# The seams into two Strassen stages of a mixer kernel: one batch kept by a copy, fewer sums, low parts on another engine

## The chip, the core and the metric

The program runs on one core of one Trainium2 chip. The metric is the time of one execution in device microseconds (us). Of the kernel before there are three timed runs and one profiled execution. In the text PE is TensorE, DVE is VectorE, ACT is ScalarE, POOL is GpSimd and SP is SyncE, whose queue issues nearly all DMAs here.

## What is computed

Attention over 4 batches of 448 tokens (12 heads of 64), then two mixers on the result, in 32-bit floats:

```python
attn = softmax(rmsnorm(q) @ rmsnorm(k).T / 8) @ v
x = attn, heads side by side                 # 4 batches of 448 x 768
u = x + (U V) mixing of the tokens           # first mixer, rank 32
x = u + relu(u @ w_ch1) @ w_ch2              # 768 -> 3072 -> 768
u = x + relu(x^T @ w_tok1) @ w_tok2          # second mixer, over tokens
out = u + relu(u @ w_ch1) @ w_ch2            # 768 -> 1536 -> 768
```

## The kernel before, in words

To keep 32-bit accuracy on the fast matmul path every operand is held as two tiles, a high part (its rounded copy) and a low part (what the rounding left). A product takes three matmuls: high by high, low by high, high by low. `split` makes the two parts: ACT copies the value to the high part, then POOL subtracts (lines 143 to 145).

The work is done in two halves: batches 0 and 1 first, then 2 and 3. This case concerns the second half, where `pair_ffn` runs the channel part of a mixer for two batches together, once for the first mixer (its name is `"a"`, 24 chunks of hidden width) and once for the second (`"b"`, 12 chunks). "Batch 0" of the change means the first of the two, `xs[0]`; `xs[1]` is the other. Both hold u transposed, 128 partitions by 6 chunks of 448 tokens. `us[0]` and `us[1]` are the split copies of the same u, named `uh, ul` and `vh, vl` inside the function. The result of each group of hidden chunks is added to `xs` in place (`second`, line 645 before), so `xs` no longer holds u once the first group is through.

Hidden chunks go two at a time (G = 2). The first group and the last are computed plainly: `plain` makes the hidden activations (tile `ps_g`, then the relu into `gs`), `second` multiplies them with the second weights (tile `ps_x`) and adds to `xs`. The groups between use Strassen's scheme over a 2 by 2 block matrix, the two batches being one dimension: `seven` makes seven products (tile `ps_p`) in place of eight. For that it needs

- four combinations of the two u, T1 to T4, once per stage (`sums`, tiles `t1` to `t4`, each with a high and a low part): T1 = u1a - u0a, T2 = u1b - T1, T3 = u1b - u1a, T4 = u0b - T2, where 0 and 1 are the batches and a and b the halves of the channels;
- four combinations of the two weight chunks, once per group (`w1_blocks`, from line 212): DVE makes the sums (lines 223 to 226, tile `w_t`), `split` makes the parts (tiles `w_a` and `w_s`).

In `sums` before, u of `xs[1]` is taken from `xs[1]` itself, while u of `xs[0]` is put together from `uh` and `ul`, since `xs[0]` has been changed by then. That costs a second operation in T1 and in T4:

```python
nc.vector.tensor_sub(t1, x[:, c], f(uh[:, c]))
nc.vector.tensor_sub(t1, t1, f(ul[:, c]))
```

The scheduler of the framework reorders what the code says: it places each engine's instructions by its own estimate of when they could run, so the order on each engine is a result, and it differs from the order of the lines. Each engine then works strictly through its list. Two places are called seams below: **seam A**, where the last batch's rank mix ends and stage "a" begins (about 1010 to 1072 us of the span), and **seam B**, where the token mix ends and stage "b" begins (about 1400 to 1458 us).

PSUM is shared out by pools: `m` has 3 buffers, `s` 2, `t` 1 and `p` 2. `ps_g` takes from `m`, and `ps_x` in `pair_ffn` in turn from `m` and `p`. A buffer of `ps_x` is freed by the DVE addition to `xs`.

Of the kernel before, what the change touches and what calls it, by code (L numbers as in the profile page):

```python
# [10 lines left out]
F32R = mybir.dt.float32r  # L11
U32 = mybir.dt.uint32
I64 = mybir.dt.int64
AF = mybir.ActivationFunctionType
# [10 lines left out]
def attention_then_two_mixers(  # L25
# [30 lines left out]
    nc = tc.nc  # L56
    P = 128
    B, H, S, D = q.shape
# [8 lines left out]
    G = 2  # L67
# [4 lines left out]
    act = ctx.enter_context(tc.tile_pool(name="act", bufs=2))  # L72
    dram = ctx.enter_context(tc.tile_pool(name="dram", bufs=1, space=DRAM))

    def f(x):
        return x.bitcast(F32)

    def mm(o, l, r, start, stop):
        nc.tensor.matmul(o, lhsT=l, rhs=r, start=start, stop=stop)  # L79
# [20 lines left out]
    pools = {"late": False}  # L100
# [7 lines left out]
    def psum(kind, shape, name):  # L108
        pool = pools[kind]
        return pool.tile(shape, F32, tag=pool.name, name=name)  # L110
# [32 lines left out]
    def split(w, hi, lo):  # L143
        nc.scalar.activation(hi, w, AF.Copy)  # L144
        nc.gpsimd.tensor_sub(lo, w, f(hi))  # L145
# [63 lines left out]
    def tmp():  # L209
        return pools["pu"].tile([P, S], F32, tag="pu", name="pu")  # L210
# [346 lines left out]
    def pair_ffn(nm, w1, w2, xs, us, after, half=None):  # L557

        n = w1.shape[1] // P
        HC = CC // 2  # L560
        (uh, ul), (vh, vl) = us

        def sums():


            ts = [act.tile([P, 2, HC, S], F32R, tag="xT", name="t1")]
            ts += [pools["tb"].tile([P, 2, HC, S], F32R, tag=f"t{i}", name=f"t{i}")
                   for i in (2, 3, 4)]
            x = xs[1]
            for c in range(HC):  # L570
                t1, t2, t3, t4 = [tmp() for _ in range(4)]
                nc.vector.tensor_sub(t1, x[:, c], f(uh[:, c]))
                nc.vector.tensor_sub(t1, t1, f(ul[:, c]))
                nc.vector.tensor_sub(t2, x[:, HC + c], t1)
                nc.gpsimd.tensor_sub(t3, x[:, HC + c], x[:, c])
                nc.vector.tensor_sub(t4, f(uh[:, HC + c]), t2)
                nc.vector.tensor_add(t4, t4, f(ul[:, HC + c]))
                for t, v_ in zip(ts, (t1, t2, t3, t4)):
                    split(v_, t[:, 0, c], t[:, 1, c])
            return {f"t{i + 1}": (t[:, 0], t[:, 1]) for i, t in enumerate(ts)}  # L580

        def plain(u, ws):
            pg = psum("m", [P, S], "ps_g")
            wh, wl = ws
            for cc in range(CC):
                fs = slice(cc * P, (cc + 1) * P)
                mm(pg, wh[:, fs], u[0][:, cc], cc == 0, False)
                mm(pg, wl[:, fs], u[0][:, cc], False, False)
                mm(pg, wh[:, fs], u[1][:, cc], False, cc == CC - 1)
            return relu(pg)  # L590

        def relu(ps):
            s = pools["g"].tile([P, 2, S], F32R, tag="g", name="gs")
            gh, gl = s[:, 0], s[:, 1]
            nc.scalar.activation(gh, ps, AF.Relu)  # L595
            nc.vector.scalar_tensor_tensor(
                gl, ps, 0.0, f(gh), op0=ALU.max, op1=ALU.subtract
            )
            return gh, gl
# [37 lines left out]
        def second(xT, gs, ws, done=None):  # L637
            for dc in range(CC):
                px = psum("mp"[dc % 2], [P, S], "ps_x")
                ds = slice(dc * P, (dc + 1) * P)  # L640
                for i, ((gh, gl), (wh, wl)) in enumerate(zip(gs, ws)):
                    mm(px, wh[:, ds], gh, i == 0, False)
                    mm(px, wl[:, ds], gh, False, False)
                    mm(px, wh[:, ds], gl, False, i == len(gs) - 1)
                nc.vector.tensor_add(xT[:, dc], px, xT[:, dc])  # L645
                if done and dc % 3 == 2:
                    done(dc // 3)
                yield
# [5 lines left out]
        def chunks(j0):  # L654
            return ([w1_chunk(nm, w1, j0 + i) for i in range(G)],
                    [w2_chunk(nm, w2, j0 + i) for i in range(G)])

        def drain(it):
            for _ in it:
                pass  # L660

        w1s, w2s = chunks(0)
        drain(second(xs[0], [plain(us[0], ws) for ws in w1s], w2s))
        b = sums()
        b.update(b11=(uh[:, :HC], ul[:, :HC]), b21=(uh[:, HC:], ul[:, HC:]),
                 b22=(vh[:, HC:], vl[:, HC:]))
        rest_ = second(xs[1], [plain(us[1], ws) for ws in w1s], w2s)
        for j0 in range(G, n - G, G):
            a = w1_blocks(nm, j0)
            gs = [[None] * 2 for _ in xs]  # L670
            for _ in seven(a, b, gs):
                next(rest_, None)
                next(rest_, None)
            drain(rest_)
            rest_ = seconds(gs, [w2_chunk(nm, w2, j0 + i) for i in range(G)])
        w1s, w2s = chunks(n - G)
# [39 lines left out]
    xs = [new_x() for _ in range(2)]  # L716
    us = [None] * 2
# [4 lines left out]
    wt, kept = [], []  # L722
    with ExitStack() as stack:
# [6 lines left out]
        def new_xo():  # L730
# [4 lines left out]
             for b, xT in zip((b0, b1), xs) for hp in range(NP)]  # L735
            + [(b, hp, (), new_xo,
                lambda dst, b=b, hp=hp: nc.sync.dma_start(xd[b][hp], dst))
# [10 lines left out]
        w1s = [w1_chunk("a", wa1, j) for j in range(G)]  # L748
# [80 lines left out]
```

## Time and profile before

| what | value |
| --- | --- |
| timed runs | 1589.35, 1595.9, 1597.39 us; median 1595.9 |
| profiled execution, its own time | 1591.42 us |
| its span, first to last instruction | 1589.4 us |
| busy: PE, DVE, ACT, POOL | 93%, 72%, 46%, 51% of the span |
| mean granted TensorE clock | 0.981 of full |

A share is busy time over the whole span. PE is busy nearly throughout, but the page's 40 slices show two dips of PE in the second half, in the slices around 1020 us and 1420 us, where POOL is at its fullest. The granted clock is 1.0 (the 2.4 GHz level) or 0.5 (the 1.2 GHz level) at any moment. A mean below 1 says for how much of a stretch the lower level was granted.

### The profile page before, as it was taken

What the parts mean: (1) busy time and instruction counts of PE and PEld (TensorE: products, weight loads), DVE (VectorE), ACT (ScalarE), POOL (GpSimd) and SP (SyncE); (2) the same over time, 40 slices, a digit from 0 to 9 for tenths busy, and PEclk for the clock granted to TensorE, in tenths of its full rate; (3) what the DMA queues carried; (4) which work ended last, traced back from release to release, by engine and by line L of the source; (5) the groups of instructions that cost most, each with busy time, mean ns of one, the idle gap of its engine ahead of it and who ended that gap; (6) DMA issues with size and microseconds to landing.
All of it is one profiled execution on the core that took longest, in us unless ns stands there. A gap on an engine that the chain in (4) does not pass through costs nothing.

```text
span 1589.4 us, 21794 instructions
## 1 busy us (share of the span) xinstructions
PE 1482.6 (93%) x7522; PEld 1283.8 (81%) x7522; DVE 1137.4 (72%) x1949; ACT 730.1 (46%) x1461; POOL 806.4 (51%) x659
## 2 busy tenths in 40 slices
PE   5999987999999999998999999689999999979998
PEld 3556566788779898897888998579999999978997
DVE  6899878998788888667857654755766664475653
ACT  5788755666556665434534334322322321332311
POOL 4567657767556564444745443662343522375320
PEclk9999989999999999999999999889999999999999
DMA  5666553556554453542415423111212111001202
GB/s 150 152 159 163 144 173 112 178 149 204 178 170 148 137 158 108 204 144 86 171 63 199 157 100 118 46 40 50 70 50 69 47 54 52 29 21 50 70 20 90
DMA packets 103373, 178.21 MB, mean 112 GB/s; under 512 B 10400, under 2 KB 79488, under 8 KB 103264
## 3 DMA queue, kind: packets, MB, share of 16 engines
q1 hardware_dynamic: 102944, 176.82, 36.0%
q8 instruction: 60, 0.98, 0.3%
q14 instruction: 49, 0.40, 0.1%
q10 hardware_dynamic: 320, 0.00, 0.0%
HBM read 107.19 MB, written 36.57 MB: 90 GB/s over the span
## 4 chain that ended last, share of the span: by engine, by line
PE 58%; DVE 15%; POOL 5%; issue 4%; DMA 3%; ACT 2%; SPq 0%; DVEq 0%; POOLq 0%; ACTq 0%
PE ps_x L79 26%; PE ps_g L79 14%; PE ps_p L79 11%; POOL w_bits L134 2%; DVE w_bits L131 2%; DVE xT L528 2%; DVE w_bits L126 2%; PE ps_u L79 2%; PE ps_t L79 2%; PE sc L79 1%; PE pv L79 1%; DVE nm L330 1%; DVE w_bits L127 1%; DVE pl L370 1%; PE pt L358 1%
## 5 line engine op out<-in xcount | busy, mean ns | idle before, releaser
L79 PE MATMUL ps_x<-gs,w 128*128 128x448 f32 x2592 | 579.8, 371 | 27.4 <-ACT gs L595 11.2
L79 PEld LDWEIGHTS ps_x<-gs,w 128*128 128x128 f32 x2592 | 484.2, 190 | 76.9 <-DVE xT L528 14.0
L79 PE MATMUL ps_g<-u,w 128*128 128x448 f32 x1584 | 347.3, 371 | 6.6 <-POOL u L438 4.3
L79 PEld LDWEIGHTS ps_g<-u,w 128*128 128x128 f32 x1584 | 295.6, 189 | 34.6 <-POOL u L438 6.3
L134 POOL TENSOR_TENSOR w_bits<-w_bits,w_round 128x768 uint32<-128x768 uint32 (+3 forms) x80 | 143.7, 1797 | 114.8 <-issue 36.3
L145 POOL TENSOR_TENSOR w<-w_bits,w 128x768 fp32r<-128x768 f32 (+3 forms) x82 | 147.7, 1809 | 87.1 <-ACT w L144 82.0
L339 POOL TENSOR_SCALAR p<-p,sm 112x448 f32<-112x448 f32 x192 | 132.0, 701 | 99.5 <-DVE sm L336 37.7
L645 DVE TENSOR_TENSOR xT<-ps_x,xT 128x448 f32<-128x448 f32 x216 | 128.5, 618 | 72.7 <-PE ps_x L79 71.2
L528 DVE TENSOR_TENSOR xT<-ps_x,xT 128x448 f32<-128x448 f32 x216 | 132.2, 617 | 40.3 <-PE ps_x L79 38.4
L145 POOL TENSOR_TENSOR w<-w 128x768 fp32r<-128x768 f32 x44 | 83.5, 1908 | 133.3 <-ACT w L144 109.2
L332 ACT ACTIVATE p<-sc,nm 112x448 f32<-112x448 f32 x192 | 121.6, 637 | 54.3 <-DVE nm L330 48.4
L145 POOL TENSOR_TENSOR w_a<-w_a 128x384 fp32r<-128x384 f32 (+1 forms) x28 | 42.9, 1531 | 167.9 <-DVE w_t L223 124.3
L616 DVE TENSOR_TENSOR pu<-ps_p,pu 128x448 f32<-128x448 f32 x98 | 58.9, 620 | 89.0 <-PE ps_p L79 84.0
L330 DVE TENSOR_REDUCE nm<-sc 112x1 f32<-112x448 f32 x192 | 116.2, 613 | 8.5 <-PE sc L79 7.6
L358 PEld LDWEIGHTS pt<-ident,p 112*112 112x112 f32 x768 | 86.4, 133 | 39.7 <-issue 19.4
L366 ACT ACTIVATE ph<-pt 112x448 fp32r<-112x448 f32 (+1 forms) x192 | 101.6, 546 | 27.1 <-PE pt L358 26.0
L358 PE MATMUL pt<-ident,p 112*112 112x112 f32 x768 | 111.2, 262 | 2.6 <-POOL p L339 1.5
L126 DVE TENSOR_SCALAR w_bits<-w_bits 128x768 f32<-128x768 f32 (+3 forms) x80 | 71.0, 888 | 47.4 <-ACT w_bits L125 47.4
L130 ACT ACTIVATE w_round<-w_raw 128x768 uint32<-128x768 uint32 (+3 forms) x80 | 69.8, 872 | 72.2 <-POOL w_bits L134 67.1
L438 POOL TENSOR_TENSOR u<-xT,u 128x448 fp32r<-128x448 f32 x48 | 61.4, 1289 | 68.7 <-ACT u L437 68.3
L370 DVE TENSOR_TENSOR pl<-pt,ph 112x448 fp32r<-112x448 f32 x144 | 87.4, 613 | 10.0 <-ACT ph L366 9.3
L125 ACT ACTIVATE w_bits<-w_raw 128x768 f32<-128x768 f32 (+3 forms) x80 | 70.0, 875 | 49.9 <-POOL w L145 35.5
(107 smaller groups left out, 2433.1 us busy)
## 6 DMA issues: line engine op xcount, KB each, us to landing
w_raw<-in_moe_w_ch_dram SPq DMA_DIRECT2D x72, 768.0 KB, 4.5
c_a<-w_bits SPq DMA_DIRECT2D x48, 384.0 KB, 3.4
ks<-hi SPq DMA_DIRECT2D x96, 112.0 KB, 2.3
kt<-lo SPq DMA_DIRECT2D x96, 112.0 KB, 2.3
w<-c_a SPq DMA_DIRECT2D x28, 384.0 KB, 3.7
c_b<-w_bits SPq DMA_DIRECT2D x24, 384.0 KB, 3.1
w_a<-c_a SPq DMA_DIRECT2D x20, 384.0 KB, 2.9
w<-c_b SPq DMA_DIRECT2D x16, 384.0 KB, 3.3
```

What stands on the lines that cost most here:

```text
L79: nc.tensor.matmul(o, lhsT=l, rhs=r, start=start, stop=stop)
L126: nc.vector.tensor_scalar_max(f(w), f(w), TINY)
L134: nc.gpsimd.tensor_tensor(w, w, r, op=ALU.add)
L145: nc.gpsimd.tensor_sub(lo, w, f(hi))
L330: nc.vector.tensor_reduce(nm, sc, axis=AX.X, op=ALU.max, negate=True)
L332: nc.scalar.activation(p, sc, AF.Exp, bias=nm, accum_out=sm[:, c % 2:c % 2 + 1])
L339: nc.gpsimd.tensor_scalar(x, x, sm[:, i:i + 1], 1.0, op0=ALU.mult, op1=ALU.mult)
L358: nc.tensor.transpose(pt[:, c * CP:(c + 1) * CP], pr[c][:, kc * CP:(kc + 1) * CP], ident[:CP, :CP],)
L366: nc.scalar.activation(ph, pt, AF.Copy)
L370: nc.vector.tensor_sub(pl, pt, f(ph))
L528: nc.vector.tensor_add(xT[:, dc], px, xT[:, dc])
L645: nc.vector.tensor_add(xT[:, dc], px, xT[:, dc])
```

## The change

Four things, all in `pair_ffn`:

- A new `keep_first` runs ahead of everything else in the stage: two DMAs on SP's queue copy `xs[0]`, as long as it is still u, into the low-part halves of the tiles of T3 and T4 (128 by 1344 floats of 4 bytes each, 672 KB a copy). The low parts proper are written over them later.
- `sums` takes u of batch 0 from that copy. Per channel chunk it has four operations where it had six, so 12 for 18 per stage; T3, which POOL made, is now made by DVE.
- The low parts of T1 to T4 are subtracted by DVE (`part`), no longer by POOL (`split`): 12 operations per stage.
- The first group's `w1_blocks` is called ahead of the plain group, and the plain hidden activations of batch 1 (`g1`) ahead of `sums`.

```diff
+        def keep_first():
+            ts = [pools["tb"].tile([P, 2, HC, S], F32R, tag=f"t{i}", name=f"t{i}") for i in (3, 4)]
+            for h, t in enumerate(ts):
+                nc.sync.dma_start(f(t[:, 1]), xs[0][:, h * HC:(h + 1) * HC])
+            return ts
...
+            def part(t, c, v_):
+                nc.scalar.activation(t[:, 0, c], v_, AF.Copy)
+                nc.vector.tensor_sub(t[:, 1, c], v_, f(t[:, 0, c]))
             for c in range(HC):
-                t1, t2, t3, t4 = [tmp() for _ in range(4)]
-                nc.vector.tensor_sub(t1, x[:, c], f(uh[:, c]))
-                nc.vector.tensor_sub(t1, t1, f(ul[:, c]))
+                t1, t2, t3 = [tmp() for _ in range(3)]
+                nc.vector.tensor_sub(t1, x[:, c], f(k3[:, 1, c]))
                 nc.vector.tensor_sub(t2, x[:, HC + c], t1)
-                nc.gpsimd.tensor_sub(t3, x[:, HC + c], x[:, c])
-                nc.vector.tensor_sub(t4, f(uh[:, HC + c]), t2)
-                nc.vector.tensor_add(t4, t4, f(ul[:, HC + c]))
+                nc.vector.tensor_sub(t3, x[:, HC + c], x[:, c])
+                t4 = tmp()
+                nc.vector.tensor_sub(t4, f(k4[:, 1, c]), t2)
                 for t, v_ in zip(ts, (t1, t2, t3, t4)):
-                    split(v_, t[:, 0, c], t[:, 1, c])
+                    part(t, c, v_)
...
         w1s, w2s = chunks(0)
+        kept = keep_first()
+        a = w1_blocks(nm, G)
         drain(second(xs[0], [plain(us[0], ws) for ws in w1s], w2s))
-        b = sums()
+        g1 = [plain(us[1], ws) for ws in w1s]
+        b = sums(kept)
...
-        rest_ = second(xs[1], [plain(us[1], ws) for ws in w1s], w2s)
+        rest_ = second(xs[1], g1, w2s)
         for j0 in range(G, n - G, G):
-            a = w1_blocks(nm, j0)
+            a = a or w1_blocks(nm, j0)
```

The code of the changed kernel is 11 to 15 lines further down: the addition of line 645 is line 656 there, the one of line 616 is 627, and the relu's lines 595 and 596 are 606 and 607. The sums of T1 to T4 are lines 584 to 588, their parts lines 579 and 580, the copies line 567.

What the scheduler makes of it, at the places that matter. First TensorE at seam A, from the last matmuls of the rank mix (`ps_u`) on; `ps_g` and `ps_x` are the plain group, `ps_p` the first Strassen products, and the numbered `t` are the tiles of T. Before:

```order
L79 MATMUL ps_x<-gs,w 128x448 x6
L79 MATMUL ps_g<-u,w 128x448 x2
L79 MATMUL ps_u<-w,xs 128x448 x6
L79 MATMUL ps_p<-u,w_a 128x448
L79 MATMUL ps_g<-u,w 128x448 x16
L79 MATMUL ps_p<-t_11373,w_s 128x448
L79 MATMUL ps_g<-u,w 128x448 x2
L79 MATMUL ps_x<-gs,w 128x448 x6
L79 MATMUL ps_p<-t_11373,w_s 128x448 x4
```

And in the changed program:

```order
L79 MATMUL ps_x<-gs,w 128x448 x6
L79 MATMUL ps_u<-w,xs 128x448 x6
L79 MATMUL ps_p<-u,w_a 128x448
L79 MATMUL ps_g<-u,w 128x448 x18
L79 MATMUL ps_x<-gs,w 128x448 x6
L79 MATMUL ps_g<-u,w 128x448 x18
L79 MATMUL ps_p<-u,w_a 128x448 x8
L79 MATMUL ps_x<-gs,w 128x448 x6
L79 MATMUL ps_p<-u,w_a 128x448 x9
```

All 36 matmuls of the plain group for batch 1 now stand behind the rank mix (before, 18 of them stood ahead of its end), and no product with a T stands among them; the first one comes 9 `ps_x` matmuls behind the last row shown.

VectorE at the same place, before (`xT_10984` is `xs[1]`, `xT_9415` is `xs[0]`; the first rows are the end of the rank mix):

```order
L436 TENSOR_TENSOR xT_10984<-ps_u_11237,xT_10984 128x448
L574 TENSOR_TENSOR pu_11377<-xT_10984,pu_11376 128x448
L436 TENSOR_TENSOR xT_10984<-ps_u_11243,xT_10984 128x448
L223 TENSOR_TENSOR w_t_11481<-w_a_11475 128x384
L224 TENSOR_TENSOR w_t_11481<-w_a_11474,w_a_11475 128x384
L576 TENSOR_TENSOR pu_11379<-u_10866,pu_11377 128x448
L572 TENSOR_TENSOR pu_11394<-xT_10984,u_10866 128x448
L225 TENSOR_TENSOR w_t_11482<-w_t_11481,w_a_11474 128x384
L577 TENSOR_TENSOR pu_11379<-pu_11379,u_10867 128x448
```

And in the changed program:

```order
L436 TENSOR_TENSOR xT_10984<-ps_u_11237,xT_10984 128x448
L436 TENSOR_TENSOR xT_10984<-ps_u_11243,xT_10984 128x448
L223 TENSOR_TENSOR w_t_11291<-w_a_11285 128x384
L224 TENSOR_TENSOR w_t_11291<-w_a_11284,w_a_11285 128x384
L225 TENSOR_TENSOR w_t_11292<-w_t_11291,w_a_11284 128x384
L226 TENSOR_TENSOR w_t_11292<-w_a_11284,w_t_11292 128x384
L656 TENSOR_TENSOR xT_9415<-ps_x_11353,xT_9415 128x448
L656 TENSOR_TENSOR xT_9415<-ps_x_11361,xT_9415 128x448
L656 TENSOR_TENSOR xT_9415<-ps_x_11369,xT_9415 128x448
L584 TENSOR_TENSOR pu_11447<-xT_10984,t3_11280 128x448
```

The additions to `xs[0]` stood ahead of the end of the rank mix and now stand behind it and behind the four weight sums: they may not write before the copy has read `xs[0]`. In the program the copy waits for the last `ps_u` matmul of seam A, since the tiles of T3 and T4 lie where the rank mix's factors lay.

GpSimd at seam A, before:

```order
L145 TENSOR_TENSOR t_11374<-pu,t_11374 128x448
L438 TENSOR_TENSOR u<-xT,u 128x448
L145 TENSOR_TENSOR w_a<-w_t,w_a 128x384
L145 TENSOR_TENSOR w_s<-w_t,w_s 128x384 x2
L575 TENSOR_TENSOR pu<-xT 128x448
L145 TENSOR_TENSOR t_11375<-pu,t_11375 128x448
L145 TENSOR_TENSOR w_a<-w_a 128x768
L145 TENSOR_TENSOR t_11372<-pu,t_11372 128x448
```

And in the changed program:

```order
L438 TENSOR_TENSOR u<-xT,u 128x448 x11
L145 TENSOR_TENSOR w_a<-w_a 128x384
L438 TENSOR_TENSOR u<-xT,u 128x448
L145 TENSOR_TENSOR w_a<-w_t,w_a 128x384
L145 TENSOR_TENSOR w_s<-w_t,w_s 128x384
L145 TENSOR_TENSOR w_a<-w_a 128x768
L145 TENSOR_TENSOR w_s<-w_t,w_s 128x384 x2
L145 TENSOR_TENSOR w<-w 128x768 x4
```

No operation of T is left on GpSimd: behind the parts of u and of the first weight blocks it has only the parts of the next weights, which wait for their DMAs.

## Rows read from the trace of the kernel before

**Rows 1.** Waits of PE, 1072.44 to 1410: us in total, times, longest.

```profile
PE ps_p L79 <- DVE xT L645: 0.4, 2, 0.2
```

**Rows 2.** Timeline of PE, seam A: start, us, what, [idle before <-releaser].

```profile
1016.79 2.94 PE L79 MATMUL ps_g<-u,w 128*128 128x448 f32 x12 [0.90 <-POOL u L438]
...
1023.42 0.47 PE L79 MATMUL ps_p<-t,w_s 128*128 128x448 f32 x1 [3.69 <-ACT w_s L144]
...
1032.28 2.61 PE L79 MATMUL ps_x<-gs,w 128*128 128x448 f32 x6 [7.74 <-ACT gs L595]
...
1051.26 4.66 PE L79 MATMUL ps_p<-t,w_a 128*128 128x448 f32 x14 [2.00 <-ACT pu L620]
...
1062.13 0.47 PE L79 MATMUL ps_p<-u,w_a 128*128 128x448 f32 x1 [1.25 <-DVE pu L616]
...
1066.24 1.08 PE L79 MATMUL ps_x<-gs,w 128*128 128x448 f32 x4 [1.08 <-DVE gs L596]
1068.59 2.25 PE L79 MATMUL ps_x<-gs,w 128*128 128x448 f32 x6 [1.27 <-DVE xT L645]
```

**Rows 3.** Timeline of PE, seam B.

```profile
1418.00 0.64 PE L79 MATMUL ps_p<-t,w_s 128*128 128x448 f32 x2 [2.50 <-ACT t L144]
...
1423.91 1.05 PE L79 MATMUL ps_g<-u,w 128*128 128x448 f32 x2 [2.22 <-POOL u L438]
1428.38 3.36 PE L79 MATMUL ps_x<-gs,w 128*128 128x448 f32 x8 [3.42 <-ACT gs L595]
...
1453.88 1.08 PE L79 MATMUL ps_x<-gs,w 128*128 128x448 f32 x4 [0.86 <-DVE gs L596]
1456.23 1.48 PE L79 MATMUL ps_x<-gs,w 128*128 128x448 f32 x6 [1.27 <-DVE xT L645]
```

**Rows 4.** Windows at half clock: length, busy PE PEld DVE ACT POOL, PEclk, DMA, GB/s.

```profile
1024.65:1038.30 13.65, 6.02 (x16) 5.38 (x17) 10.45 (x9) 5.88 (x11) 13.65 (x11) 0.50 0.00 0
1051.96:1055.37 3.41, 3.41 (x11) 3.04 (x11) 1.69 (x3) 1.04 (x2) 3.41 (x3) 0.50 0.01 5
1069.02:1072.44 3.42, 3.42 (x11) 3.03 (x10) 2.20 (x5) 0.52 (x1) 3.42 (x3) 0.50 0.00 0
...
1424.01:1434.25 10.24, 6.82 (x18) 5.55 (x19) 7.34 (x7) 4.96 (x9) 10.24 (x8) 0.50 0.05 19
```

**Rows 5.** Timeline of DVE, 1016 to 1032.

```profile
1016.20 0.95 DVE L223 TENSOR_TENSOR w_t<-w_a 128x384 f32<-128x384 f32 x1
1017.08 1.50 DVE L224 TENSOR_TENSOR w_t<-w_a 128x384 f32<-128x384 f32 x1
...
1021.34 1.48 DVE L225 TENSOR_TENSOR w_t<-w_t,w_a 128x384 f32<-128x384 f32 x1
...
1025.56 1.34 DVE L226 TENSOR_TENSOR w_t<-w_a,w_t 128x384 f32<-128x384 f32 x1
```

**Rows 6.** Tile pu: duration ns min/median/max, first and last start, forms.

```profile
L616 DVE TENSOR_TENSOR pu<-ps_p,pu x98: 608/624/626, 1051.3 to 1533.7; 128x448 f32<-128x448 f32 x98
...
L145 POOL TENSOR_TENSOR t<-pu,t x24: 1142/1486/1541, 1007.2 to 1439.3; 128x448 fp32r<-128x448 f32 x24
...
L572 DVE TENSOR_TENSOR pu<-xT,u x6: 615/1427/1575, 1004.1 to 1422.8; 128x448 f32<-128x448 f32 x6
```

**Rows 7.** Timeline of DVE, 1379.5 to 1394: `xs[0]` complete, and its first addition.

```profile
1380.05 0.62 DVE L436 TENSOR_TENSOR xT<-ps_u,xT 128x448 f32<-128x448 f32 x1
...
1391.97 1.15 DVE L645 TENSOR_TENSOR xT<-ps_x,xT 128x448 f32<-128x448 f32 x2
```

**Rows 8.** DMA issues: count, KB each, median us from issue to landing.

```profile
w_raw<-in_moe_w_ch_dram SPq DMA_DIRECT2D x72, 768.0 KB, 4.5
...
w_a<-c_a SPq DMA_DIRECT2D x20, 384.0 KB, 2.9
```

**Rows 9.** Timeline of DVE, seam B, 1395 to 1434: first and third chunk's T2.

```profile
1409.90 1.59 DVE L574 TENSOR_TENSOR pu<-xT,pu 128x448 f32<-128x448 f32 x1
...
1425.92 1.37 DVE L574 TENSOR_TENSOR pu<-xT,pu 128x448 f32<-128x448 f32 x1
```

More of the change, by code (lines that the diff above doesn't have):

```diff
@@ L561, in pair_ffn, with sums @@
         (uh, ul), (vh, vl) = us
[L563 to L568, printed above, removed]
+        def keep_first():
[3 more added lines that the diff above has]
+            return ts
+        def sums(kept):
+            k3, k4 = kept
+            ts = [act.tile([P, 2, HC, S], F32R, tag="xT", name="t1"),
+                  pools["tb"].tile([P, 2, HC, S], F32R, tag="t2", name="t2"), k3, k4]
             x = xs[1]
+            def part(t, c, v_):
+                nc.scalar.activation(t[:, 0, c], v_, AF.Copy)
+                nc.vector.tensor_sub(t[:, 1, c], v_, f(t[:, 0, c]))
             for c in range(HC):
-                t1, t2, t3, t4 = [tmp() for _ in range(4)]
-                nc.vector.tensor_sub(t1, x[:, c], f(uh[:, c]))
-                nc.vector.tensor_sub(t1, t1, f(ul[:, c]))
+                t1, t2, t3 = [tmp() for _ in range(3)]
+                nc.vector.tensor_sub(t1, x[:, c], f(k3[:, 1, c]))
                 nc.vector.tensor_sub(t2, x[:, HC + c], t1)
-                nc.gpsimd.tensor_sub(t3, x[:, HC + c], x[:, c])
-                nc.vector.tensor_sub(t4, f(uh[:, HC + c]), t2)
-                nc.vector.tensor_add(t4, t4, f(ul[:, HC + c]))
+                nc.vector.tensor_sub(t3, x[:, HC + c], x[:, c])
+                t4 = tmp()
+                nc.vector.tensor_sub(t4, f(k4[:, 1, c]), t2)
                 for t, v_ in zip(ts, (t1, t2, t3, t4)):
-                    split(v_, t[:, 0, c], t[:, 1, c])
+                    part(t, c, v_)
             return {f"t{i + 1}": (t[:, 0], t[:, 1]) for i, t in enumerate(ts)}
@@ L673, in pair_ffn @@
                 next(rest_, None)
+            a = None
             drain(rest_)
```

## The prediction

> **What bounds the kernel now.** I read the page's busy shares first. PE is busy for 93% of the span, so only time in which PE stands still or runs slowly can be won. Next come PE's waits in the long middle of the stages: from 1072.44 to 1410 us they come to 0.4 us [rows 1]. The steady groups therefore leave nothing, and the two seams are the place. Their timelines show seven waits at seam A, 0.90 + 3.69 + 7.74 + 2.00 + 1.25 + 1.08 + 1.27 = 17.9 us [rows 2], and five at seam B, 2.50 + 2.22 + 3.42 + 0.86 + 1.27 = 10.3 us [rows 3]. Last come the windows in which the granted clock was 0.50, the 1.2 GHz level, each after one or more of these waits [rows 4]. A matmul takes twice as long there, so half of PE's busy time in them is lost: (6.02 + 3.41 + 3.42) / 2 = 6.4 us at A and 6.82 / 2 = 3.4 us at B. In all 24.3 us are lost at A and 13.7 us at B. This is what the change works on, 38 us.
>
> Why PE waits: the longest wait at each seam ends with ACT's relu `gs` [rows 2, 3], and that relu stands in ACT's list behind the high parts of T, which wait for DVE's sums. Those sums are slow because POOL works beside them. With POOL busy throughout the first of these windows [rows 4], operations of DVE that read two SBUF tiles take 1.34 to 1.50 us, the first weight sum apart [rows 5]. A sum of T has a shortest time of 0.615 and a median of 1.427, while the additions that read PSUM (line 616) stay between 0.608 and 0.626 [rows 6]. Undisturbed operations start 0.54 us apart (two in 1.15 us, the second lasting 0.62) [rows 7]. So there are two prices for a T sum: 1.43 beside POOL, 0.54 without.
>
> **The change, part by part.**
>
> *Fewer sums, low parts on DVE.* DVE goes from 15 operations of T per stage to 24 (12 sums, 12 low parts), POOL from 15 to none. In POOL's list at seam A nine operations are left behind the last rank-mix matmul: three parts of u, six of the weight blocks. At 1.14 alone or 1.49 beside DVE, the prices of the like operation on T [rows 6], they last 10.3 to 13.4 us; I take 12. After that POOL only has the parts of the next weights, whose DMAs wait for PE, so DVE works at 0.54.
>
> A rule of the Trainium skill bears on these two prices. SBUF — State Buffer, section "SBUF: two separate sides", has VectorE and GpSimd share one port pair as an exclusive lock, held for a whole instruction, the other blocked. By it a contended sum would cost its own 0.62 plus POOL's 1.14, 1.76 us; the trace shows 1.34 to 1.50 [rows 5], so it agrees in direction and not in size. At 1.76 the some 12 contended operations that I count below would cost 4 us more, and the time would come to 1581; I keep the rows' 1.43.
>
> *The copy, and the new wait.* The copies wait for the last `ps_u` matmul of seam A. The additions to `xs[0]` wait for the copies and stand in DVE's list behind the four weight sums; and the three PSUM buffers of pool `m` are held by `ps_x` tiles that wait for these additions, so the first `ps_g` row of PE waits too. This is a new gap on PE. Behind the last matmul DVE has the last rank-mix addition (0.62), the four weight sums, 0.95 + 1.50 + 1.48 + 1.34 = 5.27 [rows 5], and the first addition to `xs[0]` (0.62): 6.5 us, of which one Strassen matmul fills 0.4. The trace has no copy of this kind. The nearest rows: 384 KB land in 2.9 us, 768 KB in 4.5 [rows 8]. One copy of 672 KB so takes 2.9 to 4.5 us, both together 4.5 to at most 9.0 (one after the other). The first three additions need the first copy alone, and 4.5 is under the 5.9 after which DVE comes to them, so I cost it at nothing: the weight sums cover it. Without that cover the gap would be 2.9 + 0.62 - 0.4 = 3.1 us at least and 9.0 + 0.6 - 0.4 = 9.2 at most. I take 6.1.
>
> After the gap PE has 50 matmuls (18 `ps_g`, 6 `ps_x`, 18 `ps_g`, 8 `ps_p`) that need nothing of T: 10 to 12 us (12 of them last 2.94 us, the last one's run-out included [rows 2]). It then needs the first relu. DVE has until it two more additions to `xs[0]` (1.1), three sums at 1.43 and two additions while POOL still works (5.4), then three sums at 0.54 (1.6), with ACT's copy and the relu 1.1: 9.2 us behind the first addition. The cover holds, by 1 us at least.
>
> *Clock.* The new gap is of the kind after which the 1.2 GHz level was granted. After 7.74 us of waiting it cost 3.0 us, after 2.00 us 1.7 [rows 2, 4]. I take 2.4.
>
> *The weight sums "with the plain group".* Called earlier, they still stand right behind the last rank-mix addition, as before; what is new is that they stand together and ahead of the additions. I give this part nothing of its own; its cost is in the gap above.
>
> *What stays at A.* The wait of 2.00 (and the 1.7 of the clock behind it) goes: product 1, whose ACT copy it waits for, now ends ahead of the T products. The last three waits (3.60) and their half-clock window (1.7) belong to the next group's weight sums, which the change leaves; I keep all 5.3. **Seam A: 6.1 + 2.4 + 5.3 = 13.8 left of 24.3, gain 10.5.**
>
> *Seam B.* Here `xs[0]` is complete at 1380.7 and its first addition comes at 1392.0 [rows 7], 11 us later, more than the 9.0 of both copies; on SP's queue the second-weight loads behind the first copy and the next group's behind the second wait for PE anyway. So the copies cost nothing, and there is no new gap. The relu that ends the 3.42 wait stands behind 12 of the sums (11 before). Before, they ran from 1409.9 to 1427.3 [rows 9], three additions among them, 17.4 us. Now POOL has five operations left there (two of weight blocks, three parts of u), 5.7 to 7.5 us by the prices above; I take 7: five at 1.43, seven at 0.54 and three additions at 0.54 are 12.6 us, so the relu comes 4.8 us earlier. Of the first three waits (8.1) 3.3 remain. The clock's 3.4 falls to the same 2.4 as at A. The last two waits (2.1) I keep. **Seam B: 7.8 left of 13.7, gain 5.8.**
>
> **The sum.** 10.5 + 5.8 = 16.3 us against the profiled execution's own 1591.42: 1575.1. That execution lies 4.5 us below the median of the three runs, 1595.9, and the four executions known spread from 1589.35 to 1597.39. I put the median of the changed kernel 2 us above the sum: **1577 us**. By the bounds of the copy, of the clock (1.7 to 3.0 per seam) and of the waits kept, this case reaches from 1570 to 1584.
>
> **The rivals.**
>
> 1. *DVE stays contended* (slower). 24 operations of T and 4 weight sums, 28 at 1.43, in place of 19: 9 more per seam are 12.9 us before the last T is ready, and PE has nothing else by then. At B the relu waits for one more, 1.4 us. That is 14.3 us slower, 1591.4 + 14.3 + 2 = 1608. It decides where 28 operations take as long as 19 did (27.2 us): from a mean of 0.97 us, which is when about half of them meet POOL. For it: POOL filled the whole window [rows 4]. Against: POOL's 15 operations of T per stage are gone, and nine others are left at A and five at B. The Trainium skill, Perfetto Trace Analysis, section "Optimizing Scalar/DVE Operations", speaks for it: the two engines share a read port, so moving work from one to the other might not help. The price above is from rows, and the shortest times in [rows 6] show that DVE is fast once POOL is quiet. Chance 0.06.
> 2. *The new gap takes the place of the old waits* (no change). All four weight sums at 1.5 us, both copies at 9.0 one after the other: a gap of 9.2, the 1.2 GHz level for as long as before (3.0 at A, 3.4 at B), the 2.00 wait and its 1.7 come back behind ACT's longer list, and seam B keeps 7.0 of its 8.1: A 9.2 + 3.0 + 9.0 = 21.2, B 7.0 + 3.4 + 2.1 = 12.5, gain 4.3, 1589. For it: everything behind the gap waits on one DMA that the trace has never shown. Chance 0.10.
> 3. *The copy lands very late*, say 15 us after its issue, at A alone: the gap is 15.2, 9.1 longer, gain 7.2, 1586. Beyond 22 us nothing is gained. Against: no DMA of this size class takes over 4.5 [rows 8]. Chance 0.05.
> 4. *The waits go altogether.* Only the gap remains at A (6.1, with 1.7 of clock) and 1.0 at B: gain 24.3 - 7.8 + 13.7 - 1.0 = 29, 1564. It needs the next group's weight sums to come in time, too. Chance 0.09.
>
> **How the numbers follow.** The forecast has 0.70. 0.5% of this time, about 8 us, is the least that a measurement tells from no change. Faster by more than that (below 1587.9): the forecast, case 4 and most of case 3, with a share of case 2: 0.70 + 0.09 + 0.03 + 0.04 = 0.86. Slower: case 1 less what lies near its threshold, 0.05. The rest, 0.09, is no change. The range leaves out case 1, half of case 4 and some of case 2: 1566 to 1588.
>
> **What would show it.** In the changed profile: one PE gap of 5 to 7 us at the first `ps_g` behind the rank mix, ended by DVE's addition (line 656), not by the copy; copies landing in 3 to 5 us; T sums with a median below 0.7 us; no wait on the relu (line 606) over 1 us at A; three waits of about 3.6 us together at the next group. I am wrong if T sums have a median above 1 us, if a copy lands after 6 us, or if PE's waits at the two seams together stay above 22 us.

## The result, and the profile of the changed kernel

| | before | changed |
| --- | --- | --- |
| median of the timed runs | 1596.64 us (1589.35 to 1598.82, 4 runs) | 1575.32 us (1573.31 to 1579.07, 4 runs) |
| ratio, 95% interval | | 0.9877 [0.984, 0.9914] |
| profiled execution: own time, span | 1591.42, 1589.4 us | 1573.31, 1571.2 us |
| busy: PE, DVE, ACT, POOL | 93%, 72%, 46%, 51% | 94%, 72%, 47%, 49% |

The forecast was 1577 us, with a range from 1566 to 1588. In a later comparison the changed kernel came to 1580.23 us, 0.9895 [0.9868, 0.9923] of the kernel before: the same program differs by 5 us between two comparisons.

What answers to [rows 2, 3] is PE's timeline at the two seams, with all waits over 0.35 us from the end of the rank mix on:

```profile
1017.91 5.84 PE L79 MATMUL ps_g<-u,w 128*128 128x448 f32 x18 [5.85 <-DVE xT L656]
...
1036.43 2.12 PE L79 MATMUL ps_x<-gs,w 128*128 128x448 f32 x9 [0.69 <-DVE gs L607]
...
1056.90 1.89 PE L79 MATMUL ps_p<-t,w_s 128*128 128x448 f32 x8 [1.17 <-POOL w_s L145]
...
1404.05 0.87 PE L79 MATMUL ps_p<-t,w_s 128*128 128x448 f32 x3 [0.88 <-DVE xT L436]
...
1408.77 0.47 PE L79 MATMUL ps_p<-t,w_s 128*128 128x448 f32 x1 [1.95 <-DVE t L580]
...
1411.61 1.49 PE L79 MATMUL ps_p<-t,w_a 128*128 128x448 f32 x6 [0.44 <-ACT pu L631]
...
1435.33 0.74 PE L79 MATMUL ps_p<-t,w_s 128*128 128x448 f32 x1 [2.78 <-ACT w_s L144]
```

Seam A has one long wait, the forecast gap, and two short ones: 5.85 + 0.69 + 1.17 = 7.7 us where there were 17.9. Seam B has 0.88 + 1.95 + 0.44 + 2.78 = 6.05 us where there were 10.3. The windows at half clock, against [rows 4]:

```profile
1015.25:1022.08 6.83, 4.17 (x11) 3.74 (x12) 6.80 (x10) 2.28 (x5) 6.83 (x6) 0.50 0.15 57
1435.09:1438.51 3.42, 3.18 (x8) 2.64 (x9) 2.35 (x5) 1.01 (x3) 3.09 (x3) 0.50 0.00 0
```

One is left at A, around the gap (4.17 / 2 = 2.1 us lost), and one at B, behind the wait for the next group's weights. The gap itself is made on DVE, whose timeline is this:

```profile
1011.76 0.63 DVE L436 TENSOR_TENSOR xT<-ps_u,xT 128x448 f32<-128x448 f32 x1 [0.22 <-PE ps_u L79]
1012.30 0.94 DVE L223 TENSOR_TENSOR w_t<-w_a 128x384 f32<-128x384 f32 x1
1013.16 1.48 DVE L224 TENSOR_TENSOR w_t<-w_a 128x384 f32<-128x384 f32 x1
1014.57 1.34 DVE L225 TENSOR_TENSOR w_t<-w_t,w_a 128x384 f32<-128x384 f32 x1
1015.95 1.38 DVE L226 TENSOR_TENSOR w_t<-w_a,w_t 128x384 f32<-128x384 f32 x1
1017.25 1.67 DVE L656 TENSOR_TENSOR xT<-ps_x,xT 128x448 f32<-128x448 f32 x3
```

The order is the last rank-mix addition, the four weight sums, and the first addition to `xs[0]`, with next to nothing idle between them. The view has these rows for the copies, issued at 1011.7 and 1012.3 (count, ns of the issue, first and last start; then us to landing, for these two):

```profile
L567 SPq DMA_DIRECT2D t<-xT x2: 487/540/593, 1011.7 to 1012.3; - x2
DMA to landing us min/median/max: 3.3/3.9/4.4
```

The first landed at 1011.75 + 3.3 = 1015.1, two us ahead of the addition that needs it. The T sums, against [rows 6] (ns min/median/max over both stages):

```profile
L584 DVE TENSOR_TENSOR pu<-xT,t x6: 608/618/1573, 1018.8 to 1407.6; 128x448 f32<-128x448 f32 x6
L585 DVE TENSOR_TENSOR pu<-xT,pu x6: 607/900/2257, 1020.6 to 1409.2; 128x448 f32<-128x448 f32 x6
L586 DVE TENSOR_TENSOR pu<-xT x6: 607/1023/1576, 1021.7 to 1410.2; 128x448 f32<-128x448 f32 x6
L588 DVE TENSOR_TENSOR pu<-t,pu x6: 609/830/1731, 1024.4 to 1412.4; 128x448 f32<-128x448 f32 x6
```

Over all 24 sums the median is 0.62 us; over the 30 of before it is 1.42. The means lie closer, 0.99 and 1.32, because the sums are of two kinds: 10 of the 24 still took over 1 us, where 26 of the 30 did.

The time ahead of seam A varies by up to 10 us between profiles in which the same work stands there. To compare profiles I therefore take two stretches with PE marks that every kernel has: A from the last rank mix's `ps_u` matmuls that wait for DVE's `xs` to the first transpose (`pt_x`) of the token mix, B from there to the end of the span. Before, then changed (windows: length, busy PE, PEld, DVE, ACT, POOL, PEclk, DMA, GB/s):

```profile
1002.10:1345.41 343.31, 324.62 (x1555) 295.27 (x1556) 216.05 (x314) 90.74 (x160) 148.28 (x105) 0.97 0.16 51
1345.41:1589.40 243.99, 228.00 (x1148) 207.87 (x1146) 136.79 (x208) 67.75 (x124) 94.71 (x67) 0.98 0.15 47
```

```profile
1003.23:1331.47 328.24, 319.71 (x1556) 292.44 (x1556) 215.41 (x326) 90.92 (x160) 128.03 (x90) 0.99 0.18 58
1331.47:1571.20 239.73, 227.88 (x1148) 206.38 (x1146) 137.05 (x217) 67.49 (x124) 74.85 (x52) 0.99 0.16 54
```

A is 15.1 us shorter: PE's idle time fell from 18.7 to 8.5, its busy time by 4.9, about what the clock windows lost less (6.4 us before, 2.1 now). B is 4.3 us shorter, all of it idle time (16.0 to 11.85). DVE's busy time did not change; POOL's fell by 40 us.

### The profile page after: what moved, and what is told of

Its sections match the earlier page's. It is cut to its first block, busy times and chain, and to the rows that moved or that the text cites. A ratio compares the mean times of both kernels' runs of the same rounds, so it can differ in the third digit from the quotient of the medians.

```text
span 1571.2 us, 21805 instructions
## 1 busy us (share of the span) xinstructions
PE 1479.1 (94%) x7522; PEld 1281.0 (82%) x7522; DVE 1137.1 (72%) x1967; ACT 730.8 (47%) x1461; POOL 766.9 (49%) x629
## 4 chain that ended last, share of the span: by engine, by line
PE 57%; DVE 16%; POOL 4%; issue 4%; DMA 4%; ACT 3%; SPq 0%; DVEq 0%; POOLq 0%; ACTq 0%
PE ps_x L79 26%; PE ps_g L79 13%; PE ps_p L79 10%; POOL w_bits L134 2%; DVE w_bits L131 2%; DVE xT L528 2%; DVE w_bits L126 2%; PE ps_u L79 2%; PE ps_t L79 2%; DVE nm L330 1%; PE sc L79 1%; PE pv L79 1%; DVE w_bits L127 1%; DVE pl L370 1%; POOL w L145 1%
```

## The experiments

Theory 1, on which the prediction stood, is that the gain is DVE's release from POOL, which brings a T sum from 1.43 to 0.54 us. Its rivals are theory 2, the fewer sums that the copy allows; theory 3, each of the two suffices alone; and theory 4, the order of the calls. Each row has one profile, from which its stretches are. Here are all results, with the kernel before at 1595.73 us (for the first four rows), 1598.1 (the next four) and 1595.09 (the last four):

| kernel | median us | ratio, 95% interval | stretch A | stretch B |
| --- | --- | --- | --- | --- |
| order alone | 1598.42 | 1.0002 [0.9978, 1.0027] | 345.1 | 244.3 |
| low parts alone | 1587.08 | 0.9941 [0.9921, 0.9962] | 337.4 | 243.6 |
| copy alone | 1583.43 | 0.9921 [0.9892, 0.995] | 331.3 | 240.6 |
| changed, low parts on POOL | 1579.83 | 0.9906 [0.9876, 0.9937] | 326.8 | 240.3 |
| changed, again | 1580.23 | 0.9895 [0.9868, 0.9923] | 329.7 | 239.7 |
| changed, low parts on POOL, again | 1579.54 | 0.9887 [0.9854, 0.9919] | 326.3 | 240.5 |
| changed, no copy | 1585.5 | 0.9943 [0.9915, 0.997] | 334.2 | 238.9 |
| copy free, weight sums early | 1573.93 | 0.9858 [0.9831, 0.9885] | 323.0 | 239.1 |
| copy free alone | 1582.14 | 0.9917 [0.9897, 0.9937] | 332.7 | 238.0 |
| weight sums early alone | 1573.63 | 0.9869 [0.9848, 0.9891] | 325.8 | 238.5 |
| both, low parts on POOL | 1578.27 | 0.9905 [0.9882, 0.9928] | 324.4 | 240.3 |
| both, again | 1572.56 | 0.9857 [0.9838, 0.9876] | 323.4 | 238.0 |

### The order of the calls alone

```diff
+        a = w1_blocks(nm, G)
         drain(second(xs[0], [plain(us[0], ws) for ws in w1s], w2s))
+        g1 = [plain(us[1], ws) for ws in w1s]
         b = sums()
...
-        rest_ = second(xs[1], [plain(us[1], ws) for ws in w1s], w2s)
+        rest_ = second(xs[1], g1, w2s)
...
-            a = w1_blocks(nm, j0)
+            a = a or w1_blocks(nm, j0)
...
```

> The kernel before with only the two calls moved: the first weight blocks ahead of the plain group, and the plain hidden activations of batch 1 ahead of the sums. No copy, 18 sums, low parts on POOL. If the moved calls bring part of the gain (rival: the order in the code), the time falls by the 5 us or so that the later waits at seam A shrank by, to about 1591, and PE's waits there change. If, as I think, the scheduler puts every engine's instructions where it puts them anyway, the instruction lists are those of before, the seven waits of seam A come back at 17 to 19 us, and the time is that of before, 1596 within 4 us.

It measured 1.0002 of the kernel before. Every engine's list is, row by row, that of the kernel before, and the two long waits of seam A come back (7.3 us on `gs`, 3.7 on `w_s`). In the kernel before, the moved calls do nothing by themselves. I therefore put the order of rows in the changed kernel down to the copy and to the engines of the T operations; beside the copy the moved calls were not tried apart.

### The low parts alone

```diff
-                    split(v_, t[:, 0, c], t[:, 1, c])
+                    nc.scalar.activation(t[:, 0, c], v_, AF.Copy)
+                    nc.vector.tensor_sub(t[:, 1, c], v_, f(t[:, 0, c]))
```

> The kernel before with only the low parts of T on DVE: 18 sums, no copy, T3 still made by POOL (3 operations a stage left there in place of 15). Theory 1, the gain is DVE's release from POOL: most of the gain is here, 14 us of the 20, so about 1582 with T sums near 0.6 us once POOL's parts of u are done. Theory 2, the gain is the fewer sums that the copy allows: DVE has 27 operations of T in place of 15 and gains nothing or loses, 1596 to 1605. Theory 3, both edits shorten the same chain and each alone brings most: 1580 to 1584 here and about the same with the copy alone, so that the two gains add up to much more than that of the whole change.

It measured 8.6 us below the kernel before; theory 1 had 14, and the result lies between the ranges of theories 2 and 3. These are PE's waits at seam A from the end of the rank mix on:

```profile
1019.43 2.93 PE L79 MATMUL ps_g<-u,w 128*128 128x448 f32 x12 [0.90 <-POOL u L438]
...
1026.46 0.74 PE L79 MATMUL ps_p<-t,w_s 128*128 128x448 f32 x1 [4.10 <-ACT w_s L144]
...
1033.79 1.48 PE L79 MATMUL ps_x<-gs,w 128*128 128x448 f32 x6 [2.23 <-DVE gs L597]
...
1062.23 4.25 PE L79 MATMUL ps_x<-gs,w 128*128 128x448 f32 x12 [2.12 <-DVE xT L646]
```

The 7.74 us on the relu fell to 2.23, so the low parts' move is worth something here, though DVE had 27 operations in place of 15. The wait for the first weight parts, whose sums stand among those of T on DVE, stayed (4.10).

### The copy alone

```diff
...
-                nc.vector.tensor_sub(t1, x[:, c], f(uh[:, c]))
-                nc.vector.tensor_sub(t1, t1, f(ul[:, c]))
+                nc.vector.tensor_sub(t1, x[:, c], f(k3[:, 1, c]))
...
-                nc.vector.tensor_sub(t4, f(uh[:, HC + c]), t2)
-                nc.vector.tensor_add(t4, t4, f(ul[:, HC + c]))
+                nc.vector.tensor_sub(t4, f(k4[:, 1, c]), t2)
...
```

The copy itself (`keep_first`) is that of the changed kernel.

> The kernel before with only the copy and the 12 sums: T3 and all low parts stay on POOL. DVE has 9 operations of T a stage, POOL 15. Theory 1 (release from POOL): the sums stay at about 1.4 us, little is gained, 1590 or above. Theory 2 (fewer sums): nearly the whole gain, 1576 to 1580, though POOL works as long as before. Theory 3 (either edit suffices): 1577 to 1582, with the one PE gap of about 6 us at seam A that the copy's order brings.

It measured 12.3 us below the kernel before, with the T sums on DVE as slow as ever (median 1.40 us over the 18) and POOL as busy (800.7 us). Theory 1 as the only cause falls. The 1583.43 us hit none of the three ranges and come nearest to theory 3's (1577 to 1582). But the low parts alone and the copy alone add up to 20.9 us, about the whole gain (17.9 and 21.3 us in its two comparisons), and not to much more, as theory 3 would have it. PE's waits at seam A:

```profile
1025.33 6.16 PE L79 MATMUL ps_g<-u,w 128*128 128x448 f32 x18 [5.84 <-DVE xT L656]
...
1059.71 0.47 PE L79 MATMUL ps_p<-u,w_a 128*128 128x448 f32 x1 [1.25 <-DVE pu L627]
1060.24 2.50 PE L79 MATMUL ps_x<-gs,w 128*128 128x448 f32 x11
1064.14 1.07 PE L79 MATMUL ps_x<-gs,w 128*128 128x448 f32 x4 [1.40 <-DVE gs L607]
1066.49 1.48 PE L79 MATMUL ps_x<-gs,w 128*128 128x448 f32 x6 [1.27 <-DVE xT L656]
```

The gap is there, the wait on the relu is gone, and the last three waits of [rows 2] (3.60 us) are there nearly unchanged (3.92). The copy does two things at once: it saves six sums a stage, and it holds the additions back, so that all of the plain group's 36 `ps_g` matmuls for batch 1 stand between the rank mix and the first product with a T. No kernel here has the one without the other.

### The changed kernel with the low parts on POOL

```diff
-                nc.vector.tensor_sub(t[:, 1, c], v_, f(t[:, 0, c]))
+                nc.gpsimd.tensor_sub(t[:, 1, c], v_, f(t[:, 0, c]))
```

> The changed kernel with the low parts of T back on POOL (12 operations a stage); the copy, the 12 sums and T3 on DVE stay. My prediction's reason, DVE's release from POOL, would have the T sums go back to about 1.4 us and the first relu late: 1582 to 1588, some 10 us behind the changed kernel. Theory 3 (either edit suffices): 1574 to 1578, as the changed kernel, since DVE then has 12 operations of T in place of 24 and can afford 1.4 us each.

It measured 0.9906 (1579.83 us, between the ranges of the two theories), too near to the changed kernel's 0.9877 to say more, so both ran side by side on one chip:

> The changed kernel once more, beside the next one on the same chip. No theory differs on it: 0.984 to 0.991 of the kernel before. It is here because the copy with the low parts on POOL came to 0.991 in another call, and a difference of 0.3% between two calls settles nothing.

> The changed kernel with the low parts of T on POOL, again, beside the changed kernel on the same chip. In the profiles PE's waits over 0.35 us at the two seams came to 12.4 us with the low parts on POOL and to 13.8 us with them on DVE. If the profiles are right, the two kernels take the same time within 3 us. If the medians of the separate calls are right (1579.8 and 1575.3), the low parts on DVE are worth 4 us or more, and this one is slower by that.

Side by side the changed kernel took 1580.23 us (1577.08 to 1584.09) and the one with the low parts on POOL 1579.54 (1574.13 to 1584.17): the same, as far as such spreads can tell, which is to within some 4 us. In the second profile PE's waits at seam A were 5.85 and 0.49 us, and this is what T cost on both engines:

```profile
L580 POOL TENSOR_TENSOR t<-pu,t x24: 1134/1535/1543, 1030.6 to 1426.2; 128x448 fp32r<-128x448 f32 x24
L584 DVE TENSOR_TENSOR pu<-xT,t x6: 625/1560/1578, 1025.4 to 1412.0; 128x448 f32<-128x448 f32 x6
...
L588 DVE TENSOR_TENSOR pu<-t,pu x6: 1021/1498/1582, 1029.7 to 1418.0; 128x448 f32<-128x448 f32 x6
```

The sums are as slow as before the change (median 1.43 us over the 24, against 0.62), and at seam A nobody is late for it. At seam B PE's waits are others:

```profile
1414.54 0.68 PE L79 MATMUL ps_g<-u,w 128*128 128x448 f32 x2 [2.93 <-POOL u L438]
...
1416.02 1.49 PE L79 MATMUL ps_p<-t,w_s 128*128 128x448 f32 x3 [0.80 <-POOL t L580]
```

POOL's parts of u and of T are late there, but with the low parts on DVE PE waits 1.95 us for one of those, and the sum of the waits at seam B is about the same (6.25 and 6.05 us). So of the four parts of the change, the low parts on DVE were worth nothing that these runs can tell. T3 on DVE seems worth more: this kernel differs from the copy alone by the three T3 sums a stage on DVE and by the moved calls, which did nothing in the kernel before. Its stretch A is 4.5 to 5 us shorter in two profiles, and the three late waits of 3.92 us are down to one of 0.49 to 0.64. The medians, 1583.43 and 1579.83, do not settle it: their intervals overlap. PE's list is another one there (behind the last product of the first group stand 17 of the plain group's `ps_x` matmuls in a row, where 21 stood). Whether that order, the moved calls or T3's own time does it was not tried apart.

### The changed kernel without the copy

```diff
...
-                nc.vector.tensor_sub(t1, x[:, c], f(k3[:, 1, c]))
+                nc.vector.tensor_sub(t1, x[:, c], f(uh[:, c]))
+                nc.vector.tensor_sub(t1, t1, f(ul[:, c]))
...
-                nc.vector.tensor_sub(t4, f(k4[:, 1, c]), t2)
+                nc.vector.tensor_sub(t4, f(uh[:, HC + c]), t2)
+                nc.vector.tensor_add(t4, t4, f(ul[:, HC + c]))
...
```

> The changed kernel without the copy: 18 sums from the split copies of u, all 18 of them and the 12 low parts on DVE, nothing of T on POOL. Theory 1 in full, the release from POOL: if it carries the gain, 1580 or less. The run with the low parts alone on DVE gave 0.994. From it I expect a little more here, since the three T3 go too: 0.988 to 0.993, 1577 to 1585, so that the copy is worth the rest.

It measured 0.9943, a little less of a gain than expected. POOL has nothing of T, and the sums are fast (median 0.61 us over the 36), but there are 30 operations of T on DVE. By the stretches the full release (low parts and T3) without the copy gains 9.1 us at A and 5.1 at B, the copy without any release 12.0 and 3.4, and both 15.1 and 4.3. Theory 3 holds in part: each does a large share alone, and together they bring less than their sum.

### The gap: copy or weight sums

Three kernels take the gap apart. The first takes the tiles of T3 and T4 off the rank mix's factors, by the order of the pools (and by taking the tile of T2 first, which the cut below leaves out):

```diff
-    open_pools(rest, (("xs", 4, 0), ("tb", 1, 0), ("pu", 5, 0)))
+    open_pools(rest, (("xs", 4, 0), ("pu", 5, 0), ("tb", 1, 0)))
...
```

> The changed kernel with only the tiles of T3 and T4 placed off the rank mix's factors, so that the copy waits for no matmul; the first weight sums stay where they are. If the copy sets the gap at seam A (rival), the gap shrinks from 5.85 us to about what the weight sums alone make, and the time falls by some us. If the weight sums in DVE's list set it and the copy is hidden behind them, as the prediction has it, the copy lands some 5 us or more ahead of the first addition, the gap stays at 5.8 us, and the time is that of the changed kernel, within 3 us.

It measured 0.9917 against the changed kernel's 0.9895 and 0.9877: no gain. These are the copies' rows, the last weight sum, the additions and PE's gap:

```profile
L567 SPq DMA_DIRECT2D t<-xT x2: 487/542/596, 1004.4 to 1004.9; - x2
DMA to landing us min/median/max: 4.0/4.5/5.1
```

```profile
1021.39 1.37 DVE L226 TENSOR_TENSOR w_t<-w_a,w_t 128x384 f32<-128x384 f32 x1
1022.68 1.67 DVE L656 TENSOR_TENSOR xT<-ps_x,xT 128x448 f32<-128x448 f32 x3
```

```profile
1023.35 6.49 PE L79 MATMUL ps_g<-u,w 128*128 128x448 f32 x18 [5.85 <-DVE xT L656]
```

Both copies had landed by 1004.9 + 5.1 = 1010.0, 12 us ahead of the addition, and the gap is the same to the hundredth. The weight sums set it. The second kernel moves only these, into tiles of the pool of `gs`, where they need not wait for the rank mix's factors:

```diff
-            pools["xs"].tile([P, 2, HD], F32, tag="xs", name="w_t") for _ in range(2))]
+            (f(pools["g"].tile([P, 2, S], F32R, tag="g", name="w_t"))[:, :, :HD] if first
+             else pools["xs"].tile([P, 2, HD], F32, tag="xs", name="w_t")) for _ in range(2))]
...
```

> The changed kernel with only the first weight sums moved, to tiles of the pool of gs, so that they run before the rank mix ends; the copy still waits for the rank mix's last matmul. Its landing, 3.3 us for the first half, is then uncovered: the gap should be 2.5 to 4 us in place of 5.85, and the time 1 to 4 us below the changed kernel. Rival, the weight sums were not what held the additions: the gap stays at 5.8.

It measured 0.9869. Beside each other on one chip the two placements came to 1582.14 us (only the copy) and 1573.63 (only the weight sums). Now the copy's landing does show, on DVE and on PE:

```profile
1023.26 1.69 DVE L657 TENSOR_TENSOR xT<-ps_x,xT 128x448 f32<-128x448 f32 x3 [2.79 <-DMA t<-xT]
```

```profile
1023.94 3.91 PE L79 MATMUL ps_g<-u,w 128*128 128x448 f32 x18 [2.16 <-DVE xT L657]
```

The gap is 2.16 us, a little under the 2.5 to 4 expected, with no half clock behind it. With the weight parts early, nine Strassen matmuls (2.11 us) stand ahead of the gap, where one stood. The third kernel has both together:

> The changed kernel with two placements changed: the tiles of T3 and T4 no longer lie where the rank mix's factors lay, so the copy waits for no matmul, and the sums of the first weight blocks are written to tiles of the pool of gs, so that they can run before the rank mix ends. The gap of 5.85 us on PE and its half-clock window (2.1 us lost) are the four weight sums and the copy standing between the last rank-mix addition and the first addition to batch 0. If that is so, both go and no wait takes their place: 6 to 8 us faster than the changed kernel, some 1568. Rival: the gap only hid the T sums, the relu is then late instead (2 to 4 us back), and the time falls by 3 us or less.

> The faster kernel once more, beside the one before on the same chip: 0.983 to 0.989 of the kernel before, and no wait of PE over 1 us at seam A ahead of the second group of Strassen products.

It measured 0.9858 and 0.9857, the first time 6.3 us below the changed kernel beside it (1573.93 and 1580.23), with 6 to 8 expected. It has the lowest medians of all, but the second one, 1572.56, is not clear of the 1573.63 of the weight sums early alone beside it: what the copy's place adds to theirs is shown by the gap that is gone, not by the time. In the second profile PE's first wait over 0.35 us behind the rank mix ends 36 us after it, at the next group's weights:

```profile
1054.67 0.47 PE L79 MATMUL ps_p<-t,w_s 128*128 128x448 f32 x1 [2.20 <-ACT w_s L144]
1055.76 2.88 PE L79 MATMUL ps_p<-t,w_s 128*128 128x448 f32 x8 [0.62 <-POOL w_s L145]
```

The last kernel is this version with the low parts on POOL (the same edit as above):

> The faster kernel with both placements changed, and the low parts of T back on POOL. In the changed kernel it made no difference where the low parts are (1580.2 and 1579.5 us on the same chip). One theory: it never does, since 12 sums leave DVE enough time; then the same time as the kernel beside it, within 3 us. The other: it was the gap of 5.85 us that gave DVE the time for slow sums; with the gap gone the sums at 1.2 to 1.5 us are late again, PE waits for the relu or for T by 3 to 6 us at seam A, and this one is slower by 3 to 6 us.

It measured 5.7 us slower than the kernel beside it (1578.27 and 1572.56). The waits are back at seam A, and the last line shows one at seam B:

```profile
1033.13 1.08 PE L79 MATMUL ps_x<-gs,w 128*128 128x448 f32 x4 [1.59 <-DVE gs L608]
...
1038.13 1.27 PE L79 MATMUL ps_x<-gs,w 128*128 128x448 f32 x5 [0.47 <-ACT gs L607]
...
1041.27 2.29 PE L79 MATMUL ps_x<-gs,w 128*128 128x448 f32 x10 [1.87 <-DVE gs L608]
...
1414.22 0.67 PE L79 MATMUL ps_g<-u,w 128*128 128x448 f32 x2 [2.94 <-POOL u L439]
```

So in the changed kernel the low parts on DVE were worth nothing at seam A because PE stood in the gap while the slow sums ran; without the gap 3.9 us of waits are back. What that costs in time is less certain than the 5.7 us. By the stretches the kernel with the low parts on POOL is only 1.0 us longer at A and 2.3 at B than the second profile of the kernel beside it (1.4 and 1.2 against the first); at A the half-clock window behind the next group's weights (1.7 us lost) is missing in exchange. And at seam B, where neither kernel has a gap, PE waits 2.94 us for POOL's part of u. I read the price as some 3 to 6 us, and not all of it as the gap's.

## Why the prediction was right, and where it was not

| term, us left | forecast | measured |
| --- | --- | --- |
| A: the new gap | 6.1 | 5.85 |
| A: clock around it | 2.4 | 2.1 |
| A: later waits, with their clock | 5.3 | 0.69 + 1.17 = 1.9 |
| B: the first waits | 3.3 | 0.88 + 1.95 + 0.44 = 3.3 |
| B: clock | 2.4 | 1.6 |
| B: the last waits | 2.1 | 2.8 |
| sum | 21.6 | 17.5 |

- **The bound and the place** were right: PE's waits at the two seams. The two stretches together fell by 19.3 us, the profiled span by 18.2; the forecast was 16.3. By the rows of the table the gain would be 38.0 - 17.5 = 20.5.
- **The gap** was right in size, cause and cover. It is ended by DVE's addition, its cause is the four weight sums in DVE's list, and the copy, which landed in 3.3 and 4.4 us, lies hidden behind them: a copy that landed 12 us ahead left the gap at 5.85, and with the sums away it showed at 2.16 us (the prediction's 3.1 at the least without that cover had one Strassen matmul ahead of the gap, not nine). The bounds for the copy were read wrongly, though: the 2.9 and 4.5 us of [rows 8] are medians, and "no DMA of this size class takes over 4.5" is false, since 38 of the 72 loads of 768 KB took longer, up to 7.4 us. All of these stand ahead of seam A; the copies themselves took 3.2 to 5.1 us in all kernels. The cover held with 2 us to spare, and a landing like the slowest of those loads would have outlasted it.
- **The clock** came out near the forecast at A. A half-clock window costs a little less than the half that I took: in it matmuls of 448 columns started 0.37 us apart, at the full clock 0.203, so about 45% of PE's busy time is lost, before and after alike.
- **"What stays at A" failed.** I kept 5.3 us as belonging to the next group's weight sums. The rows themselves named DVE's additions and a relu part [rows 2]. The waits stayed with the copy alone and went when T3 and the calls were moved too, with another order on PE; the weight blocks' own share is 1.17. The row is 3.4 of the 4.1 us by which less was left than forecast.
- **"Fewer sums, low parts on DVE" gave the wrong reason.** The T sums did go to 0.62, as forecast (below 0.7). But the sum of the gain does not hang on it: with the low parts on POOL the sums take 1.43 and the time is the same, so that on this point the forecast came true for another reason than its own. Two prices for a sum were right; that the dearer one would make the relu late, with 12 sums and the gap in front, was not so at seam A. That the cover "holds, by 1 us at least" was thus too careful.
- **Seam B**: its relu wait, 3.42 us [rows 3], is gone, as forecast. That its first waits came out at 3.3 us is luck in part: the forecast had the old ones shortened, while the 2.50 and 2.22 us for T and u are gone and 0.88 us for the token mix's addition, 1.95 for a low part on DVE and 0.44 for ACT's copy of the first product stand there, none of which the prediction has. The stretch gained 4.3 us where 5.8 was forecast: its last waits grew by 0.7, and PE's busy time is unchanged (228.00 and 227.88) though the half-clock window lost 1.6 us in place of 3.4. Some of that was spent again further on at the full granted clock: 241 matmuls from 1467.68 us on took 48.69 us before, and 242 from 1448.73 us on 49.60 in the changed kernel (last section).
- **The weight sums "with the plain group"**: the call's place in the code is indeed worth nothing (1.0002); the place of their tiles was worth some 4 us by the stretches (A 325.8, against 328.2 and 329.7; B 238.5, against 239.7), while the intervals of the ratios overlap (0.9869 against 0.9895 and 0.9877).
- **Rivals**: neither DVE's contention (1) nor the gap in the old waits' place (2) nor a late copy (3) came. Of (4), the waits that go altogether, the later waits at A came true for the larger part.

On the two rules weighed: in the profile with the low parts on POOL, the two rows of sums shown have medians of 1.56 and 1.50 us and POOL's parts one of 1.54, where the shortest took 0.63 and 1.13. By the Trainium skill, SBUF — State Buffer, section "SBUF: two separate sides", I estimate 0.63 + 1.13 = 1.76 us for a sum that waits out a whole operation of POOL. The medians stay below that, which agrees in direction. They do not refute the size, as the prediction had it: by the same rule a sum that comes upon an operation already running waits only for the rest of it. Single sums reached 1.73 us in that profile and 2.26 in the changed kernel, there beside an operation of POOL of 1.88. The Trainium skill, Perfetto Trace Analysis, section "Optimizing Scalar/DVE Operations", says that moving work between the two engines might not help. Here it did not help in the changed kernel (1580.23 and 1579.54 us) and did once the gap was gone (1578.27 and 1572.56).

## What to carry to other kernels

Slow operations are worth something only where someone waits for them: look for the chain behind the wait, and ask of each part of a change whether the wait goes without it. When a new gap appears, find which of its two covers sets it by freeing one at a time; here the place of a tile in SBUF (whose old owner it must wait for) was worth 6 us (1580.23 and 1573.93 side by side), and the place of a call in the code nothing. A part that is worth nothing beside a gap can be worth something once the gap is gone, so try it there again.

## What was not expected of the hardware

The same work ahead of the mark of stretch A took 1002.1 to 1012.2 us in the profiles. In the two below, windows at half clock make much of the difference: in all 27 us of them stand ahead of the mark before the change, 41 us in the kernel with the weight sums early, and PE is busy 8.3 us longer with as many matmuls:

```profile
0.00:1002.10 1002.10, 929.98 (x4821) 780.62 (x4821) 784.60 (x1428) 571.60 (x1178) 563.42 (x487) 0.99 0.49 149
```

```profile
0.00:1011.32 1011.32, 938.32 (x4820) 785.94 (x4821) 784.23 (x1429) 574.43 (x1182) 570.50 (x493) 0.98 0.49 147
```

This is as large as the effects studied here, and lies outside of what was changed; it is why the stretches are compared beside the medians.

The stretches have a variation of their own. Where the granted clock is 1.00, PE's matmuls of 448 columns start 202.7 ns apart in some parts of a profile and 206.7 in others, for tens to hundreds of us at a time. In the kernel with only the copy free 206.7 holds for most of stretch A, and in the changed kernel's first profile for about a quarter of it. Taking 4 ns for each such matmul, I estimate that it adds 1.2 to 5.5 us to stretch A, 4.6 of them in the 332.7 us of the copy free alone. What sets it no run here shows, and a difference of 3 us or less between two stretches should not be read without looking at it.

A wait of 5.85 us brought the 1.2 GHz level each time, in six profiles, while the one of 2.16 us did not. The length of the wait alone does not decide: 2.00 us did before the change [rows 2, 4], and so did 2.27 us, with 0.61 close behind, in the very profile of the 2.16.
